# Dropping waits in the attention periods and spreading the weight sums of a threshold attention and squared-ReLU kernel

## The chip, the core and the metric

The kernel runs on one core of a Trainium2 chip. The metric is the device time of one execution in microseconds, given as the median of several runs. The engines of the core work side by side, each through its own queue in order: TensorE (PE in the profile, PEld its weight loads), VectorE (DVE), ScalarE (ACT), GpSimd (POOL), and SyncE (SP), which issues DMAs.

## The reference

Attention of 8 batches with 8 heads, sequences of 576 rows and heads of 64, in float32: scores are q kᵀ / 8; scores below the row's maximum less tau (0.02) are masked; then the softmax and the product with v. The heads' outputs side by side are x, 4608 rows of 512. Then comes a feed-forward block:

```
h = np.maximum(x @ w_in, 0.0)      # w_in 512 x 2048
out = h * h @ w_out                # w_out 2048 x 512
```

## The kernel before

Both weights come as float64; the kernel converts them to float32 itself. Three stages follow one another.

**Attention.** Two heads of a batch make a pair, 32 pairs in all. A pair has four units of 128 query rows, and the last 64 rows of two neighbouring pairs make a shared ninth unit, the rest unit (`units`, 276; in it `t == FULL`). So there are 144 units, and `period(p)` (618) works on two of them at a time, A = 2p and B = 2p + 1, in a software pipeline: p runs from -2 to 74 (1046), with scores and softmax of units in period p and their product with v two periods later. A period is a list of named steps, written by hand: `PLAIN` (593) from p = 35 on, `CONVERTING` (596) for 2 to 34, in which the weights are fetched and converted. Each engine's queue gets its instructions in the order of the list. The steps that matter here:

- `SA`, `SB`: scores of A and of B on PE (`scores`, 423; line 434), 512 main columns and 64 rest columns per head. They are written to the six banks of the PSUM tile `sc`: the main columns of a unit with an even number to banks 0 and 5, of an odd one to 2 and 3, the rest columns to 1 and 4.
- `topA1` and so on: row minima of the negated scores on VectorE (452). `leastA`, `leastB`: the threshold, a tiny operation on POOL (459). `powA0` and so on: the exponentials on ScalarE (462). `maskA0` and so on: mask and row sum on VectorE (467), which waits for `leastA` or `leastB`. `over` (474, POOL) and `inv` (477, VectorE): the reciprocal of the sums. `spread` (517, POOL) widens it.
- `U`, `V`, `W` and `eU`, `eV`, `eW`: transposes of the weights on PE (379) and their copies on ScalarE (524). `W` and `eW` use banks 2 and 3 of `sc`.
- `PV` (533): the product with v on PE, into the start of banks 0 and 5. `x` (652 on VectorE, 654 on ScalarE) takes it from there, `xs` (669, POOL) scales the second half and stores it to DRAM as xT.
- `T` and `eT`: some of the next pairs' q or k rows are transposed on PE (397) into banks 1 and 4 and evicted by ScalarE (402 and 410) into the buffers qT, kT and qR. `TURNS` (487) says in which period. qT has a ring of 3 buffers (`Q_RING`), kT and qR of 4 (`K_RING`). A rest unit reads qR and kT, other units qT and kT.
- `s1`, `s2`: one step each of the sums of the weights (`sums_step`, 571), on POOL: `s1` in every plain period, `s2` in even ones.

**Which waits are kept.** The framework orders any two instructions that it takes to meet in a buffer. Since all attention PSUM is one tile, `touch` (354) is called for each instruction on it, and takes the order away from pairs on different banks (`declare_no_dep`), unless they may meet in SBUF: `MEET` (352) names such kinds. There, a pair of kinds with keys (numbers of pairs) that differ by a multiple of one of the rings named keeps its wait. Before the change, scores and the evictions of turned rows are one kind each, and they keep their wait if the keys differ by a multiple of 3 or of 4.

**Sums.** The feed-forward block multiplies by a recursive scheme with 7 products in place of 8, used twice: 49 products of quarter-sized blocks of blocks, whose operands are sums of blocks. For w_in these are 44 sums of 128x512 tiles in the buffer `wall` (`sums`, 249), as a generator that makes one sum each time it is asked. For the first 512 tokens, x needs 12 more (`prepare_x`, 790), loaded from DRAM in periods 40 to 43 (`load_x`, 762, called in 1048). Before the change these 12 come behind the 44.

**Hidden layers.** Nine steps of 512 tokens (`hidden_layer`, 829), each of 49 products on PE (841) with the combinations on VectorE and POOL (125) and the squares on ScalarE; g is stored to DRAM. After each product a tick comes, 49 in a layer (`also`, 1150). In ticks, `chain_out` (1115) also makes the sums of w_out: 44 chains, each a load, four small subtractions on POOL (122, by `minus`) at its ticks 6 to 9 and a store at tick 10; `CHAINS` (1069) gives their starts, six ticks apart. Their SBUF is loaded over by `load_g` (1140) at the start of the last layer, and `reload` (1058) then brings the sums of w_out into `wall`.

**Output layers.** Nine more steps with 49 products each (976).

Of the kernel before, what the change touches and what calls it, by code (L numbers as in the profile page):

```python
# [14 lines left out]
AF = mybir.ActivationFunctionType  # L15
# [33 lines left out]
def kernel(  # L49
# [25 lines left out]
    nc = tc.nc  # L75
# [5 lines left out]
    FULL = S // P  # L81
# [3 lines left out]
    BANK = 512  # L85
    MAIN = FULL * P
    STEP = 512
    NSTEP = B * S // STEP
# [149 lines left out]
    def convert6(m):  # L238
# [7 lines left out]
        if m >= 16:  # L246
            nc.sync.dma_start(out=slot_of(*chunks[m][1:3]), in_=a.bitcast(FP32))

    def sums(W, which, at):

        first = [at[a][b] for a in range(2) for b in range(2)]

        def inner(m, kinds):
            for op, o, x, y in kinds:
                to = W[m, o] if o == y else weight_tile(W, m, o)
                yield op(nc.gpsimd, to[:, :], W[m, x][:, :], W[m, y][:, :])

        early = which[0:3]
        for m in (1, 2):
            yield from inner(m, early)  # L260
        for op, o, x, y in which:
            for k_ in first:
                to = W[o, k_] if o == y else weight_tile(W, o, k_)
                yield op(nc.gpsimd, to[:, :], W[x, k_][:, :], W[y, k_][:, :])
        for m in OUTER:
            yield from inner(m, which[3:] if m in (1, 2) else which)

# [12 lines left out]
    NU = len(units)  # L280
# [68 lines left out]
    behind = mybir.DependencyInfo(mybir.DependencyClass.Sync, mybir.DependencyReason.DATA)  # L349

    Q_RING, K_RING, W_RING = 3, 4, 2
    MEET = (("scores", "turned", (Q_RING, K_RING)), ("values", "weights", (W_RING,)), ("x", "weights", (W_RING,)))

    def touch(what, made, at, size, key=0):

# [34 lines left out]
    def turn(i, which, spots, other=None):  # L390

        nat, to = loaded.pop((i, which)), places(i)
        of = [nat[:, t, :] for t in range(FULL)] + ([loaded.pop((i, 2))] if which else [])
        for t, x in enumerate(of):
            for r, (spot, at) in enumerate(spots):
                rows = ds(r * HALF, HALF)
                made = nc.tensor.transpose(spot[:, ts(t, HALF)], x[rows, :], ident[rows, rows])
                touch("turns", made, at, BANK)
        half = FULL * HALF

        def scaled(to, spot):
            touch("turned", nc.scalar.activation(out=to, in_=spot[0], func=AF.Identity, scale=qscale[:, :]), spot[1], BANK, i)  # L402

        def then():
            part = lambda r, x, n: (spots[r][0][:, ds(x, n)], spots[r][1])
            if which:
                for r, n in ((0, half), (1, half + REST)):
                    spot = part(r, 0, n)
                    copy_by = other if r and other else nc.scalar.copy
                    touch("turned", copy_by(to[1][:, ds(r * half, n)], spot[0]), spot[1], BANK, i)  # L410
# [12 lines left out]
    def scores(n, rest):  # L423

        of, t = units[n]
        at_k, count = (MAIN, REST) if rest else (0, MAIN)
        for j in range(2):
            first = n % 2 != j
            to = (3 * j + 1) * BANK + first * (BANK - REST) if rest else (3 * j + 2 * first) * BANK
            for c in range(2):  # L430
                rows, at = ds(j * D, D), ds(c * HALF, HALF)
                qT, kT, qR = turned[of[c]]
                lhs = qT[rows, ds((c * FULL + t) * HALF, HALF)] if t < FULL else qR[rows, :]
                made = nc.tensor.matmul(  # L434
                    sc[at, ds(to, count)], lhs, kT[rows, ds(at_k, count)], start=True, stop=True
                )
                touch("scores", made, to, count, of[c])

    def softmax(n):

# [69 lines left out]
    def widen(m):  # L510

        if m not in wT:
            wT[m] = sb.tile([P, (2 * CH + 2) * P], FP32, tag="wT", bufs=W_RING, name="wT")
        one = smalls.pop(m)[:, 3, 0:1]
        wide = bass.AP(tensor=one.tensor, offset=one.offset, ap=[one.ap[0], [1, 2], [2, 2], [0, D]])
        to = wT[m][:, ds(SCALE_AT * P, 2 * P)].rearrange("p (j u d) -> p j u d", j=2, u=2)
        nc.gpsimd.tensor_copy(out=to, in_=wide)
# [42 lines left out]
    def has(n):  # L560
        return 0 <= n < NU
# [4 lines left out]

    def sums_due(p):

        return p > max(starts) and not converts(p)

    def sums_step():
        while summing and next(summing[0], 0) == 0:
            summing.popleft()

    def ask(every=True):

# [7 lines left out]
    def converts(p):  # L584
        return is_wide and (has_chunk(p) or has_chunk(p - 1))
# [4 lines left out]
    def begun(n):  # L590
        return starts.get(n)

    PLAIN = """
        fetch U SA topA1 over s1 s2 topA0 SB topB1 inv eU powA1 V topB0 leastA spread PV powA0 maskA1 leastB maskA0 eV T powB1 x maskB1 powB0 xs maskB0 eT W eW
    """.split()
    CONVERTING = """
        fetch c1 T SA topA1 c3 topA0 U eU powA1 SB topB0 over topB1 powA0 c4 powB0 PV eT inv leastA maskA1 x powB1 leastB spread V eV maskA0 W maskB0 c5 c6 eW maskB1 xs c2
# [20 lines left out]
    def period(p):  # L618
# [66 lines left out]
        def every(key):  # L685
# [12 lines left out]
            "s1": lambda: sums_due(p) and sums_step(), "s2": lambda: sums_due(p) and p % 2 == 0 and sums_step(), "fetch": lambda: fetch(begun(p + 2)),  # L698
        }
        steps["spread"] = lambda: has(2 * m + 2) and widen(m + 1)  # L700
        for times in (4, 8, 14):
            steps[f"id{times}"] = lambda times=times: keep_busy(times)
        steps["over"] = lambda: do(a, "over")
# [314 lines left out]
    with tc.manual_schedule():  # L1018
        with ExitStack() as stack:
# [26 lines left out]
            for p in range(-2, NU // 2 + 3):  # L1046
                period(p)
                if X_FIRST <= p < X_FIRST + 4:
                    load_x(0, XPARTS[p - X_FIRST :][:1])
                if p == X_FIRST + 4:  # L1050
                    summing.append(prepare_x(0, lambda op, out, x, y: op(nc.gpsimd, out, x, y)))
            for _ in range(60):
                sums_step()
            ask()
        b_pool = ctx.enter_context(tc.tile_pool(name="b", bufs=2, space=PSUM))
        banks = ctx.enter_context(tc.tile_pool(name="banks", bufs=1, space=PSUM))
# [9 lines left out]
        halves_ = [(m, k, h) for m, k in blocks_out[EARLY:] for h in range(2)]  # L1066
        chains = [((0, RAW.index(k)), c) for k in RAW for c in range(4)]
        chains += [((1, made_at(m)), c) for c in range(4) for m in OUTER]
        CHAINS = [49 * n + 6 * c for n in range(NSTEP - 1) for c in range(n == 0, 6)][0 : len(chains)]
        QUARTER = BANK // 4  # L1070
        two = lambda t: t.rearrange("p (k o) -> p k o", k=2)
        raw_out = {}
# [61 lines left out]
        for n in range(NSTEP):  # L1134
# [14 lines left out]

            def also(m, at):  # L1150
                i = OUTER.index(m)
                convert_out(n, 7 * i + at)
                chain_out(n, 7 * i + at)
                if not last:
                    if 2 <= i <= 5 and at < 6:
                        next(xsums)
                    return
                spread(work.get(i, []), at)
                if 7 * i + at > 9:
                    reload(7 * i + at - 10)  # L1160
# [80 lines left out]
```

## Time and profile before

| what | value |
|---|---|
| median of 3 runs | 1295.47 us (1295.32 to 1295.79) |
| profiled execution | 1293.22 us, its span 1291.4 us |
| granted TensorE clock | 1.000 |
| PE busy | 1259.7 us, 98% of the span |
| VectorE / ScalarE / POOL busy | 996.2 / 855.5 / 909.8 us |
| DMA | 192.05 MB, mean 149 GB/s |

The span runs from the first to the last instruction. A row of the timeline gives start, length, engine, line, operation, output<-input, and count; what stands in brackets is the engine's idle time before it and what ended that. A row of the groups gives line, engine, operation, shapes and count, then busy time in us and the mean of one in ns, then idle time before and what ended it. A row of busy time by stretch gives the stretch and its length, then for PE, PEld, VectorE, ScalarE and POOL the busy us with the number of instructions, then the clock, the share of the DMA engines and GB/s. A row of waits gives who waited for whom, total us, how often, and the longest.

### The profile page before, as it was taken

How to read it: one execution, taken by the hardware profiler on the slowest of the kernel's cores; microseconds unless marked ns; L12 is line 12 of the kernel's file. 1: busy time of each engine (PE TensorE's matmuls, PEld its weight loads, DVE VectorE, ACT ScalarE, POOL GpSimd, SP SyncE). 2: the span in 40 equal slices, each digit the busy share in tenths (PEclk: the TensorE clock that was granted, in tenths of full speed). 3: DMA queues.
4: the chain of work that ended last, by engine and by line, in shares of the span. 5: the costliest groups of instructions: out<-in, count | busy, mean ns of one | idle time of the engine just before them, and what ended most of it. 6: DMA issues, size and time to landing. Idle time of an engine off the chain costs nothing.

```text
span 1291.4 us, 46350 instructions
## 1 busy us (share of the span) xinstructions
PE 1259.7 (98%) x18627; PEld 1124.3 (87%) x18627; DVE 996.2 (77%) x2425; ACT 855.5 (66%) x1536; POOL 909.8 (70%) x1102
## 2 busy tenths in 40 slices
PE   8999999999999999999999999999999999999998
PEld 6666666667676668999999999999999999999998
DVE  6999999999999995787788778777745654665463
ACT  6999999999999994756675667576523432343240
POOL 2566565666666664887898789668777867776775
PEclk9999999999999999999999999999999999999999
DMA  6555666534333423556655665489545314422411
GB/s 157 148 146 155 166 188 187 147 87 111 88 79 88 97 43 87 185 172 212 199 185 180 214 196 173 149 320 387 197 149 164 106 63 160 164 83 86 160 34 34
DMA packets 247032, 192.05 MB, mean 149 GB/s; under 512 B 97184, under 2 KB 195488, under 8 KB 246816
## 3 DMA queue, kind: packets, MB, share of 16 engines
q1 hardware_dynamic: 245360, 188.63, 48.5%
q8 instruction: 147, 2.41, 0.8%
q10 hardware_dynamic: 1456, 0.44, 0.1%
q14 instruction: 69, 0.57, 0.1%
HBM read 116.65 MB, written 72.35 MB: 146 GB/s over the span
## 4 chain that ended last, share of the span: by engine, by line
PE 61%; ACT 1%; DVE 1%; DMA 0%; issue 0%; POOL 0%; ACTq 0%; DVEq 0%; POOLq 0%
PE ph L841 30%; PE po L976 29%; PE sc L533 1%; PE sc L434 1%; DMA g<-arena 0%; ACT c L787 0%; ACT arena L820 0%; ACT arena L821 0%; PE pt L379 0%; ACT arena L524 0%; DVE arena L452 0%; DVE arena L125 0%; DVE arena L122 0%; POOL arena L122 0%; DVE arena L467 0%
## 5 line engine op out<-in xcount | busy, mean ns | idle before, releaser
L125 POOL TENSOR_TENSOR arena<-arena 128x512 f32<-128x512 f32 (+1 forms) x314 | 378.0, 1224 | 122.7 <-DVE arena L125 105.9
L976 PE MATMUL po<-wall,arena 128*128 128x128 f32 x3528 | 394.7, 275 | 1.4 <-ACT arena L753 1.4
L976 PEld LDWEIGHTS po<-wall,arena 128*128 128x128 f32 x3528 | 394.3, 192 | 1.8 <-ACT arena L753 1.8
L841 PE MATMUL ph<-arena,wall 128*128 128x128 f32 x3528 | 394.2, 275 | 0.5 <-DVE arena L652 0.5
L841 PEld LDWEIGHTS ph<-arena,wall 128*128 128x128 f32 x3528 | 394.0, 192 | 0.6 <-ACT arena L654 0.6
L125 DVE TENSOR_TENSOR arena<-ph,arena 128x512 f32<-128x512 f32 x378 | 256.5, 689 | 86.1 <-PE ph L841 65.7
L122 POOL TENSOR_TENSOR arena<-arena 128x128 f32<-128x128 f32 (+2 forms) x314 | 255.1, 814 | 52.4 <-DMA arena<-w 36.3
L462 ACT ACTIVATE arena<-arena 128x576 f32<-128x576 f32 x288 | 228.4, 889 | 21.2 <-DVE arena L452 21.2
L125 DVE TENSOR_TENSOR arena<-po,arena 128x128 f32<-128x128 f32 x378 | 108.5, 290 | 168.6 <-PE po L976 164.4
L467 DVE SCALAR_TENSOR_TENSOR arena<-arena 128x576 f32<-128x576 f32 x288 | 227.3, 818 | 2.9 <-POOL arena L459 2.0
L452 DVE TENSOR_SCALAR_CACHE_REDUCE arena<-sc 128x576 f32<-128x576 f32 x288 | 204.6, 752 | 14.5 <-ACT arena L524 6.9
L787 ACT COPY c<-arena 128x512 f32<-128x512 f32 (+1 forms) x303 | 173.9, 581 | 49.4 <-DVE arena L122 41.2
L533 PEld LDWEIGHTS sc<-arena 64*64 64x64 f32 x5760 | 144.4, 133 | 44.3 <-DVE arena L452 42.2
L122 DVE TENSOR_TENSOR arena<-arena,c 128x512 f32<-128x512 f32 (+1 forms) x267 | 175.1, 664 | 5.6 <-ACT c L787 4.0
L434 PE MATMUL sc<-arena 64*64 64x64 f32 (+1 forms) x2304 | 168.0, 414 | 4.6 <-ACT arena L402 2.7
L533 PE MATMUL sc<-arena 64*64 64x128 f32 (+1 forms) x5760 | 160.5, 262 | 10.1 <-DVE arena L452 6.1
L524 ACT COPY arena<-pt 128x1024 f32<-128x1024 f32 x144 | 161.7, 1123 | 2.0 <-PE pt L379 1.9
L753 ACT COPY arena<-po 128x128 f32<-128x128 f32 x63 | 16.7, 265 | 186.7 <-PE po L976 183.9
L379 PEld LDWEIGHTS pt<-ident,arena 64*128 64x128 f32 x2304 | 83.1, 138 | 43.1 <-ACT arena L524 35.1
L753 ACT COPY arena<-ph 128x512 f32<-128x512 f32 x63 | 36.7, 582 | 122.0 <-PE ph L841 121.5
L434 PEld LDWEIGHTS sc<-arena 64*64 64x64 f32 x2304 | 60.6, 133 | 52.5 <-issue 26.3
L379 PE MATMUL pt<-ident,arena 64*128 64x64 f32 x2304 | 100.8, 227 | 4.0 <-ACT arena L524 3.6
(49 smaller groups left out, 962.7 us busy)
## 6 DMA issues: line engine op xcount, KB each, us to landing
g<-arena SPq DMA_DIRECT2D x144, 256.0 KB, 2.7
arena<-g SPq DMA_DIRECT2D x144, 256.0 KB, 4.3
w<-arena SPq DMA_DIRECT2D x60, 256.0 KB, 2.4
wall<-w SPq DMA_DIRECT2D x49, 256.0 KB, 5.2
arena<-w SPq DMA_DIRECT2D x44, 256.0 KB, 3.6
arena<-in_v_dram SPq DMA_DIRECT2D x32, 288.0 KB, 3.9
out_dram<-arena SPq DMA_DIRECT2D x70, 128.0 KB, 3.0
arena<-in_q_dram SPq DMA_DIRECT2D x64, 128.0 KB, 3.8
```

The source lines that it names most:

```text
L122: e.tensor_tensor(out=out, in0=x, in1=y, op=ALU.subtract)
L125: e.tensor_tensor(out=out, in0=x, in1=y, op=ALU.add)
L379: made = nc.tensor.transpose(pt[:, r, ts(slot, HALF)], of[rows, :], ident[rows, rows])
L434: made = nc.tensor.matmul(sc[at, ds(to, count)], lhs, kT[rows, ds(at_k, count)], start=True, stop=True)
L452: made = nc.vector.tensor_scalar(out=s[:, j, :], in0=sc[:, ds(at, S)], scalar1=1.0, scalar2=None, op0=ALU.mult, op1=ALU.min, accum_out=nmx ...
L462: nc.scalar.activation(out=w[:, :, j, :], in_=of(j), func=AF.Exp, bias=nmx[:, j : j + 1], scale=-1.0)
L467: nc.vector.scalar_tensor_tensor(out=w[:, :, j, :], in0=of(j), scalar=thr[:, j : j + 1], in1=w[:, :, j, :], op0=ALU.is_le, op1=ALU.mult, a ...
L524: touch("weights", nc.scalar.copy(joined(to), whole(pt, 0, count)), at, 2 * BANK, m)
L533: made = nc.tensor.matmul(sc[ds(u * D, D), ds(5 * j * BANK + row, count)], loaded_v[i][rows, (c - (u != j)) % CH, :], wT[m][rows, ds(weigh ...
L787: nc.scalar.copy(c, y)
L841: nc.tensor.matmul(to[:, j, :], W_IN[m, k][:, ts(j, P)], of[k][:, m - 1, :], start=(not more and j == 0), stop=True, skip_group_check=True,)
L976: nc.tensor.matmul(to, g[:, j, :], w[:, j, :], start=(not more and j == 0), stop=(j == 3), skip_group_check=True)
```

## The change

It has three parts. The kinds are told apart: scores of a unit that reads qT are "q scores" and those of a rest unit "scores"; evictions are "turned q" or "turned k" (kT and qR). Each pair of kinds keeps its wait only by the ring that it really shares, and "scores" with "turned q" none. The plain list loses `s2`, so POOL makes one sum in each period from 35 to 71, and the 12 sums of x go ahead of what is left of the 44. Of those, 25 are then made in the periods; four more are made by VectorE in period 72 behind `inv` (`sV`), four by VectorE after that period, and the last 11 by POOL in the first hidden layer, in ticks 0 to 6, 9, 12, 15 and 18. The chains of the first hidden layer start at tick 18 instead of 6, two fewer in that layer, and all later ones come two places (twelve ticks) later.

```diff
+    by = [nc.gpsimd]
...
-                yield op(nc.gpsimd, to[:, :], W[m, x][:, :], W[m, y][:, :])
+                yield op(by[0], to[:, :], W[m, x][:, :], W[m, y][:, :])
...
-    MEET = (("scores", "turned", (Q_RING, K_RING)), ("values", "weights", (W_RING,)), ("x", "weights", (W_RING,)))
+    MEET = (("q scores", "turned q", (Q_RING,)), ("scores", "turned k", (K_RING,)), ("q scores", "turned k", (K_RING,)), ("values", "weights", (W_RING,)), ("x", "weights", (W_RING,)))
...
+        kind = "turned k" if which else "turned q"
...
-                touch("scores", made, to, count, of[c])
+                touch("q scores" if t < FULL else "scores", made, to, count, of[c])
...
-        return p > max(starts) and not converts(p)
-
-    def sums_step():
-        while summing and next(summing[0], 0) == 0:
-            summing.popleft()
+        return max(starts) < p < NU // 2 and not converts(p)
+
+    def sums_step(e=nc.gpsimd, times=1):
+        by[0] = e
+        for _ in range(times):
+            while summing and next(summing[0], 0) == 0:
+                summing.popleft()
...
-        fetch U SA topA1 over s1 s2 topA0 SB topB1 inv eU powA1 V topB0 leastA spread PV powA0 maskA1 leastB maskA0 eV T powB1 x maskB1 powB0 xs maskB0 eT W eW
+        fetch U SA topA1 over s1 topA0 SB topB1 inv sV eU powA1 V topB0 leastA spread PV powA0 maskA1 leastB maskA0 eV T powB1 x maskB1 powB0 xs maskB0 eT W eW
...
+        last = p == NU // 2
+        steps["sV"] = lambda: last and sums_step(nc.vector, 4)
...
+                if p == NU // 2:
+                    sums_step(nc.vector, 4)
                 if p == X_FIRST + 4:
-                    summing.append(prepare_x(0, lambda op, out, x, y: op(nc.gpsimd, out, x, y)))
-            for _ in range(60):
-                sums_step()
+                    summing.appendleft(prepare_x(0, lambda op, out, x, y: op(nc.gpsimd, out, x, y)))
...
-        CHAINS = [49 * n + 6 * c for n in range(NSTEP - 1) for c in range(n == 0, 6)][0 : len(chains)]
+        CHAINS = [49 * n + 6 * c for n in range(NSTEP - 1) for c in range(3 if n == 0 else 0, 6)][0 : len(chains)]
...
+                tick = 7 * i + at
+                if n == 0 and (tick < 7 or tick % 3 == 0):
+                    sums_step()
+                assert tick < 27 or not summing
```

More of the change, by code (lines that the diff above doesn't have):

```diff
@@ L263, in sums @@
                 to = W[o, k_] if o == y else weight_tile(W, o, k_)
-                yield op(nc.gpsimd, to[:, :], W[x, k_][:, :], W[y, k_][:, :])
+                yield op(by[0], to[:, :], W[x, k_][:, :], W[y, k_][:, :])
         for m in OUTER:
@@ L399, in turn @@
         half = FULL * HALF
+        kind = "turned k" if which else "turned q"
         def scaled(to, spot):
-            touch("turned", nc.scalar.activation(out=to, in_=spot[0], func=AF.Identity, scale=qscale[:, :]), spot[1], BANK, i)
+            touch(kind, nc.scalar.activation(out=to, in_=spot[0], func=AF.Identity, scale=qscale[:, :]), spot[1], BANK, i)
         def then():
@@ L409, in then @@
                     copy_by = other if r and other else nc.scalar.copy
-                    touch("turned", copy_by(to[1][:, ds(r * half, n)], spot[0]), spot[1], BANK, i)
+                    touch(kind, copy_by(to[1][:, ds(r * half, n)], spot[0]), spot[1], BANK, i)
                 scaled(to[2], part(0, half, REST))
@@ L697, in period @@
             "c5": lambda: convert5(begun(p - 1)), "c6": lambda: convert6(begun(p - 1)),
-            "s1": lambda: sums_due(p) and sums_step(), "s2": lambda: sums_due(p) and p % 2 == 0 and sums_step(), "fetch": lambda: fetch(begun(p + 2)),
+            "s1": lambda: sums_due(p) and sums_step(), "fetch": lambda: fetch(begun(p + 2)),
         }
         steps["spread"] = lambda: has(2 * m + 2) and widen(m + 1)
+        last = p == NU // 2
+        steps["sV"] = lambda: last and sums_step(nc.vector, 4)
         for times in (4, 8, 14):
```

## The prediction

> **What bounds the kernel now.** I read the page first, for the engines' shares, then the busy time by stretch, then the waits of TensorE, and last the timeline at single periods.
>
> ```profile
> span 1291.4 us, 46350 instructions
> PE 1259.7 (98%) x18627; PEld 1124.3 (87%) x18627; DVE 996.2 (77%) x2425; ACT 855.5 (66%) x1536; POOL 909.8 (70%) x1102
> ```
> ```profile
> 252.35:482.97 230.62, 223.60 (x5747) 160.40 (x5743) 218.84 (x647) 214.70 (x363) 152.42 (x236) 1.00 0.37 86
> 497.40:541.00 43.60, 43.60 (x391) 43.60 (x392) 33.21 (x53) 23.50 (x43) 30.63 (x39) 1.00 0.49 149
> 848.00:892.00 44.00, 44.00 (x397) 44.00 (x396) 31.81 (x48) 26.23 (x48) 30.31 (x25) 1.00 1.02 375
> ```
>
> TensorE (PE) is busy 1259.7 of 1291.4 us, so 31.7 us is all that taking waits away could win. The first stretch is the 36 plain attention periods (p = 35 to 70): PE works 223.60 of 230.62 us there and idles 7.0. The other two are the first and the last hidden layer, where PE never stops: nothing can be won there, only lost. So the change is judged in the plain periods, and its costs are sought wherever it puts work.
>
> A period starts when PE begins the scores of unit A (line 434):
>
> ```profile
> 252.35 2.18 PE L434 MATMUL sc<-arena 64*64 64x512 f32 x32
> ...
> 284.83 2.18 PE L434 MATMUL sc<-arena 64*64 64x512 f32 x32 [0.67 <-ACT arena L402]
> 291.12 2.33 PE L434 MATMUL sc<-arena 64*64 64x512 f32 x32
> 297.19 2.18 PE L434 MATMUL sc<-arena 64*64 64x512 f32 x32
> 303.76 2.18 PE L434 MATMUL sc<-arena 64*64 64x512 f32 x32 [0.18 <-DVE arena L652]
> 310.05 2.33 PE L434 MATMUL sc<-arena 64*64 64x512 f32 x32
> ...
> 482.97 2.18 PE L434 MATMUL sc<-arena 64*64 64x512 f32 x32 [0.33 <-DVE arena L652]
> ```
> ```profile
> PE sc L434 <- ACT arena L402: 2.7, 4, 0.7
> PE sc L434 <- DVE arena L652: 1.6, 7, 0.3
> ```
>
> The second fence holds PE's waits in the plain periods, all of them: four of about 0.67 us on ScalarE's eviction of turned q rows (402), and seven of up to 0.33 us on VectorE's x (652), which reads bank 0 before scores overwrite it. From 284.83 to 291.12 is 6.29 us, from 303.76 to 310.05 again 6.29: the length when PE waits for nothing and turns rows. From 291.12 to 297.19, where nothing is turned, it is 6.07. These are PE's floors. Rows are turned up to p = 67, except in 41, 50 and 59, so of the 36 periods 30 have the first floor and 6 the second: 188.7 + 36.4 = 225.1 us against 230.6. **At most 5.5 us** is to be had by that count, and by all idle time 7.0.
>
> **Part 1: the waits.** 284.83 starts p = 40, whose unit A is the shared rest unit of pairs 16 and 17. The q rows turned just before are those of pair 19: 19 - 16 = 3, a multiple of Q_RING, so the old rule keeps a wait. But a rest unit reads qR and kT, not qT, and its first matmuls write banks 0 and 5, not the banks 1 and 4 that the eviction empties. The same meeting comes once in nine plain periods, at p = 40, 49, 58 and 67: the four waits above.
>
> ```profile
> 283.50 0.66 PE L379 MATMUL pt<-ident,arena 64*128 64x64 f32 x16
> ```
> ```profile
> 283.95 0.83 ACT L402 ACTIVATE arena<-sc,qscale 128x256 f32<-128x256 f32 x2
> ```
> ```profile
> 283.59 0.28 DVE L652 TENSOR_TENSOR arena<-sc,arena 128x128 f32<-128x128 f32 x1
> ```
>
> The eviction ends at 284.78, and PE starts 0.05 later. Next in line are PE's own transposes, done at 284.16, and x, done at 283.87; so the scores can start at 284.17, 0.66 earlier. The rest columns in banks 1 and 4, a real meeting, follow their 512-column matmuls by 0.9 us, after 284.78. The new rule drops the old wait and keeps qT by 3 and kT by 4. Four times 0.66 is **-2.6 us**; bounds 0 (the wait is another) and -2.7.
>
> **Part 2: one sum a period.** POOL makes two sums in even periods and one in odd ones, between the small operation `over` and the threshold `leastA`, for which VectorE's first mask waits.
>
> ```profile
> 305.59 1.28 POOL L122 TENSOR_TENSOR wall<-wall 128x512 f32<-128x512 f32 x1
> ...
> 311.65 2.52 POOL L122 TENSOR_TENSOR wall<-wall 128x512 f32<-128x512 f32 x2
> 314.15 0.29 POOL L459 TENSOR_SCALAR arena<-arena,tau_p 128x2 f32<-128x2 f32 x1
> ```
> ```profile
> 305.23 0.76 DVE L452 TENSOR_SCALAR_CACHE_REDUCE arena<-sc 128x576 f32<-128x576 f32 x1
> 308.01 0.81 DVE L467 SCALAR_TENSOR_TENSOR arena<-arena 128x576 f32<-128x576 f32 x1
> 311.51 0.76 DVE L452 TENSOR_SCALAR_CACHE_REDUCE arena<-sc 128x576 f32<-128x576 f32 x1 [0.27 <-ACT arena L524]
> 314.48 0.92 DVE L467 SCALAR_TENSOR_TENSOR arena<-arena 128x576 f32<-128x576 f32 x1
> ```
>
> In the odd period 43 the mask starts 2.78 us after the first row minimum (305.23 to 308.01), and VectorE has 0.27 us free before the next minimum. In the even period 44 it starts 2.97 after (311.51 to 314.48), just behind `leastA`, and takes 0.92 instead of 0.81: 0.3 us late, as much as VectorE had free. Then x is late, and PE waits at 652. All seven of those waits stand at the end of an even period; of these the fences show 303.76 (after 42) and 482.97 (after 70). With one sum every period should run like an odd one. The visible waits are 1.6 us, the rest up to the ceiling 5.5 - 2.6 = 2.9. Odd periods are not all at the floor, so I take **-2.4 us**; bounds 0 (VectorE stays late for another reason) and -2.9, with all idle time -4.3.
>
> **What is late next.** The twelve x sums move ahead of the weight sums, to p = 45 to 56. Their last load is issued by the period before:
>
> ```profile
> 316.33 0.54 SPq L774 DMA_DIRECT2D arena<-xT  x1
> ```
> ```profile
> DMA to landing us min/median/max: 3.2/3.6/4.0
> ```
> ```profile
> 318.22 1.28 POOL L122 TENSOR_TENSOR wall<-wall 128x512 f32<-128x512 f32 x1
> 319.48 0.29 POOL L459 TENSOR_SCALAR arena<-arena,tau_p 128x2 f32<-128x2 f32 x1
> ...
> 320.82 0.79 POOL L459 TENSOR_SCALAR arena<-arena,tau_p 128x2 f32<-128x2 f32 x1 [0.22 <-DVE arena L452]
> ```
> ```profile
> 320.64 0.81 DVE L467 SCALAR_TENSOR_TENSOR arena<-arena 128x576 f32<-128x576 f32 x1
> ```
>
> Landing is at 316.33 + 3.6 = 319.9, and the first x sum needs that very part, where a weight sum now starts at 318.22. POOL, in order, holds `leastA`, the copy that widens the reciprocals and `leastB` behind it: `leastA` ends at 319.9 + 1.28 + 0.29 = 321.5 instead of 319.8, the mask starts then instead of at 320.64, 0.9 late, of which VectorE's slack takes 0.2. **+0.7 us** once; bounds 0 (an earlier landing) and 1.1 (landing after 4.0). SP's queue gets no other step in these periods.
>
> **Part 3: the boundary.** Eight sums go to VectorE, four after the reciprocal of p = 72 and four after the x of that period. Behind them in its queue stand the two last x (652); the last one frees the banks for which the first hidden product waits.
>
> ```profile
> 490.73 0.18 DVE L477 RECIPROCAL arena<-arena 128x4 f32<-128x4 f32 x1 [0.36 <-POOL arena L474]
> 493.47 0.29 DVE L652 TENSOR_TENSOR arena<-sc,arena 128x128 f32<-128x128 f32 x1 [2.56 <-PE sc L533]
> 496.93 0.29 DVE L652 TENSOR_TENSOR arena<-sc,arena 128x128 f32<-128x128 f32 x1 [3.17 <-PE sc L533]
> ```
> ```profile
> L125 DVE TENSOR_TENSOR arena<-ph,arena 128x512 f32<-128x512 f32 x378 | 256.5, 689 | 86.1 <-PE ph L841 65.7 <-ACT arena L753 5.4 <-POOL arena L125 4.7
> ...
> L125 DVE TENSOR_TENSOR arena<-arena 128x128 f32<-128x128 f32 x3 | 0.9, 293 | 0.2
> ```
>
> The trace has no 128x512 sum on VectorE with both inputs in SBUF. The nearest row has one from PSUM, 0.69 us; above it stands POOL's 1.28. I take 0.69. Four are 2.76 against 2.56 free, and the next four 2.76 against 3.17; together 5.5 against 5.7. **+0.1 us**; bounds 0 and, by 1.28, 10.2 - 5.7 = +4.5.
>
> ```profile
> 491.72 0.40 POOL L517 COPY arena<-arena 128x256 f32<-128x256 f32 x1
> ...
> 493.80 0.46 POOL L669 TENSOR_TENSOR arena<-arena 128x128 f32<-128x128 f32 x1 [1.68 <-ACT arena L654]
> ```
>
> Something speaks against this place. `leastB` at 320.82 takes 0.79 us beside VectorE's masks, which read two inputs in SBUF as the sums would; the same operation at 319.48 takes 0.29. If the sums and POOL's two operations above stand in each other's way, VectorE loses up to 0.40 + 0.46 = 0.9: 6.4 against 5.7, +0.7 instead of +0.1. The Trainium skill, "SBUF — State Buffer", section "Who interferes with whom", has this as a rule: a VectorE instruction with two SBUF inputs and a GpSimd instruction that reads SBUF exclude each other, whichever starts first. The trace agrees with that, 0.79 against 0.29.
>
> **Part 4: the first hidden layer.** Eleven sums go to POOL there, seven in the first seven ticks and four at ticks 9, 12, 15 and 18, and two chains of four small subtractions leave it for the end of layer 8.
>
> ```profile
> 508.24 1.27 POOL L125 TENSOR_TENSOR arena<-arena 128x512 f32<-128x512 f32 x1 [10.47 <-DVE arena L125]
> ```
> ```profile
> L122 POOL TENSOR_TENSOR arena<-arena 128x128 f32<-128x128 f32 x176 | 80.6, 459 | 42.0 <-DMA arena<-w 36.3
> ```
> ```profile
> L841 PE MATMUL ph<-arena,wall 128*128 128x128 f32 x3528 | 394.2, 275 | 0.5 <-DVE arena L652 0.5
> ```
>
> POOL stands idle for 10.47 us up to its first addition of the layer: room for seven sums of 1.28 (9.0). The other four are 5.1 us where eight subtractions of 0.46 (3.7) leave; the 1.4 more fits into what is left of the stretch's idle time, 43.6 - 30.6 - 10.5 = 2.5. Nine layers take 394.2 us, so one takes 43.8 and a tick, a forty-ninth of it, 0.89; the weights made here are first read at tick 28, ten ticks after the last sum. **0 us**; the cover is POOL's idle time, and without it the four sums would cost up to 5.1. The chains, twelve ticks later, end at tick 34 of the eighth layer, 13 us before the last layer's loads. 0 as well.
>
> **Sum:** -2.6 - 2.4 + 0.7 + 0.1 = -4.2 us. The profiled execution took 1293.22 us, its span 1291.4; the median of the runs shown is 1295.47, 2.25 more. I take the difference as the same on both: 1289.0 for the profiled one, **1291.3 us** for the median.
>
> **Rivals.**
> *VectorE stays the bound.* If even periods are long for another reason (rows turned, ACT's copies), part 2 gives nothing: -2.6 + 0.8 = -1.8, 1293.7 us. For it: VectorE is busy 218.84 of 230.62 us. Against it: the 0.27 us free in odd periods. Chance 0.14.
> *The wait stays.* If the four waits are no ring waits, or another takes their place at once, only part 2 is left: -2.4 + 0.8 = -1.6, 1293.9 us. Against it: pairs 16 and 19, banks 0 and 5, and just four of them. Chance 0.08.
> *Products wait for sums.* The other side: the old rule shows that waits are kept between instructions which touch different places of one buffer. If the tensor `wall`, which POOL now writes while PE reads it, does the same, each product of the first 19 ticks waits for the sum issued beside it. Seven of 1.28 in seven ticks of 0.89 cost 9.0 - 6.2 = 2.8, four more up to 5.1: -4.2 + 7.9 = +3.7, 1299.2 us. It ends slower from 4.2 us of such waits on. Against it: in the last hidden layer DMAs reload this tensor under PE, which is busy 44.00 of 44.00 us. Chance 0.08.
> *The boundary.* If VectorE and POOL stand in each other's way there, +0.7 instead of +0.1: -3.6, 1291.9 us. For it: 0.79 against 0.29 for `leastB`. Against it: what POOL does there is short and off VectorE's queue for most of the 5.7 us. Chance 0.04. This is what the Trainium skill's rule, cited in part 3, would give.
>
> **How the numbers follow.** The forecast has 0.66, its own range 1290.0 (the ceiling 5.5) to 1292.5. The range 1289.8 to 1294.2 reaches over the first two rivals and leaves out the slower one. A measurement tells about 0.2%, 2.6 us, from no change: forecast and boundary count as faster, 0.70; the first two rivals as same, 0.22; the third as slower, 0.08.
>
> **What would show it.** Right: no wait of 434 on 402 among PE's waits of the plain periods; few on 652; 226 us instead of 230.6 from p = 35 to p = 71; one mask 0.9 late at p = 45; 0.69 for the eight sums; PE without a pause in the first hidden layer. Wrong: PE waiting in 841 for POOL, a last x later than its PV, or plain periods that still alternate.

## The result and the profile after

The changed kernel takes 1290.93 us in the median of 6 runs (1288.99 to 1292.73), the kernel before 1295.63 in 6 runs beside them (1294.82 to 1298.75). The ratio is 0.996 with a 95% interval of 0.9946 to 0.9975, so some 3 to 7 us less. The forecast was 1291.3.

The page of the changed kernel, its span and the busy time of the engines:

```profile
span 1290.4 us, 46352 instructions
PE 1261.3 (98%) x18627; PEld 1127.2 (87%) x18627; DVE 998.5 (77%) x2433; ACT 854.9 (66%) x1536; POOL 897.4 (70%) x1094
```

This profiled execution took 1292.20 us, only 1.0 less than that of before, though the medians lie 4.7 apart. So the spans of the two must not be compared as wholes; the trace has to be read by stage. Lines after the change: 402 is now 406, 434 is 438, 459 is 463, 467 is 471, 517 is 521, 652 is 658, 841 is 849; in the experiments made from the kernel before (waits alone, second sum late, two sums in every period) those from 434 to 652 stand two further on, such as 436, 461, 469 and 654. The plain periods 35 to 70 and the first hidden layer, by the view of busy time by stretch:

```profile
256.12:481.79 225.67, 224.52 (x5746) 162.41 (x5742) 216.27 (x647) 214.29 (x362) 126.64 (x218) 1.00 0.38 88
496.20:540.00 43.80, 43.80 (x392) 43.80 (x393) 33.37 (x53) 23.64 (x43) 41.01 (x42) 1.00 0.40 124
```

The plain stretch fell from 230.62 to 225.67 us: **4.95 us less**; no other stage got shorter by more than 0.02. PE idles 1.15 us there (225.67 - 224.52) where it idled 7.0. In the first hidden layer POOL now works 41.0 us and PE still never stops. PE's waits in the plain stretch, all of them, and three starts of periods (39, 40 and 42):

```profile
PE sc L438 <- DVE arena L658: 0.2, 1, 0.2
```
```profile
281.25 2.33 PE L438 MATMUL sc<-arena 64*64 64x512 f32 x32
287.48 2.31 PE L438 MATMUL sc<-arena 64*64 64x512 f32 x32
...
299.84 2.18 PE L438 MATMUL sc<-arena 64*64 64x512 f32 x32
```

No wait on the eviction is left, and one of 0.2 us on x where there were seven. Period 39 lasts 6.23 us (281.25 to 287.48) instead of 6.98.

Where the rest of the profiled execution's time went: periods 1 to 34, whose code the change hardly touches, took 242.17 us (13.95 to 256.12) instead of 238.78. PE's waits there name one part of the cause, loads of q and k rows that land late:

```profile
PE sc L399 <- DMA arena<-in_q_dram: 2.1, 4, 1.1
...
PE sc L399 <- DMA arena<-in_k_dram: 0.4, 1, 0.4
```

The profile of before has no such wait. The other part is the granted clock, the share of its full speed at which TensorE is let run. Period 31 of the changed kernel, and a piece of it, by the view of busy time by stretch, where the clock is the third number from the end:

```profile
225.69:233.29 7.60, 7.50 (x146) 5.13 (x145) 4.67 (x16) 5.61 (x12) 3.71 (x7) 0.78 0.90 248
226.83:230.24 3.41, 3.41 (x48) 1.96 (x43) 1.55 (x5) 2.21 (x4) 1.34 (x4) 0.50 0.88 241
```

For 3.41 us TensorE ran at half speed, and the period took 7.60 us where it took 6.28 before, at a clock of 1.00. Over the twelve kernels profiled here, all with nearly the same code in this stage, it took 238.8 to 242.4 us, and before happened to be the shortest of all. Most of that spread goes with the clock in periods 1 and 2: they took 13.6 us in the three executions with a clock of 1.00 there, 15.0 to 15.1 in the five with 0.89, and 16.4 to 16.5 in the four with 0.79. The other 32 periods took 225.1 to 225.9 us in ten of the twelve, 227.3 with sixteen sums on VectorE and 228.6 in the changed kernel.

### The profile page after: what moved, and what is told of

Its sections match the earlier page's. It is cut to its first block, busy times and chain, and to the rows that moved or that the text cites. A ratio compares the mean times of both kernels' runs of the same rounds, so it can differ in the third digit from the quotient of the medians.

```text
span 1290.4 us, 46352 instructions
## 1 busy us (share of the span) xinstructions
PE 1261.3 (98%) x18627; PEld 1127.2 (87%) x18627; DVE 998.5 (77%) x2433; ACT 854.9 (66%) x1536; POOL 897.4 (70%) x1094
## 4 chain that ended last, share of the span: by engine, by line
PE 64%; DMA 2%; DVE 1%; ACT 1%; issue 0%; POOL 0%; SPq 0%; ACTq 0%; DVEq 0%; POOLq 0%
PE ph L849 30%; PE po L984 29%; PE sc L537 2%; PE sc L438 2%; DMA wall<-w 1%; PE pt L381 1%; DMA g<-arena 0%; PE sc L381 0%; PE sc L399 0%; DVE arena L456 0%; ACT c L795 0%; ACT arena L528 0%; DVE arena L125 0%; DVE arena L122 0%; POOL arena L125 0%
## 5 line engine op out<-in xcount | busy, mean ns | idle before, releaser
L849 PE MATMUL ph<-arena,wall 128*128 128x128 f32 x3528 | 394.4, 275 | 0.5 <-DVE arena L658 0.5
L466 ACT ACTIVATE arena<-arena 128x576 f32<-128x576 f32 x288 | 224.3, 858 | 16.7 <-DVE arena L456 16.7
L537 PEld LDWEIGHTS sc<-arena 64*64 64x64 f32 x5760 | 144.8, 133 | 44.3 <-DVE arena L456 40.4
L438 PE MATMUL sc<-arena 64*64 64x64 f32 (+1 forms) x2304 | 170.6, 417 | 0.3 <-DVE arena L658 0.2
L528 ACT COPY arena<-pt 128x1024 f32<-128x1024 f32 x144 | 157.4, 1093 | 3.6 <-PE pt L381 3.6
L438 PEld LDWEIGHTS sc<-arena 64*64 64x64 f32 x2304 | 62.8, 133 | 47.0 <-issue 22.6
```

The source lines that it names most:

```text
L438: made = nc.tensor.matmul(sc[at, ds(to, count)], lhs, kT[rows, ds(at_k, count)], start=True, stop=True)
L466: nc.scalar.activation(out=w[:, :, j, :], in_=of(j), func=AF.Exp, bias=nmx[:, j : j + 1], scale=-1.0)
L528: touch("weights", nc.scalar.copy(joined(to), whole(pt, 0, count)), at, 2 * BANK, m)
L537: made = nc.tensor.matmul(sc[ds(u * D, D), ds(5 * j * BANK + row, count)], loaded_v[i][rows, (c - (u != j)) % CH, :], wT[m][rows, ds(weigh ...
L849: nc.tensor.matmul(to[:, j, :], W_IN[m, k][:, ts(j, P)], of[k][:, m - 1, :], start=(not more and j == 0), stop=True, skip_group_check=True,)
```

## The experiments

The theory: two separate gains in the plain periods, one from four needless waits, one from a second POOL sum that holds the threshold back; everything else is covered. The rivals are those of the prediction. All plain stretches below run from the start of period 35 to that of period 71, read from each kernel's trace as above; before has 230.62 and after 225.67. Each is of one execution; four kernels that have the same code up to the end of the stretch (the changed one, sixteen sums, nineteen sums, chains not shifted) agree to 0.5 us. The medians of the whole kernel are coarser: by them alone, sums alone is not told from before, as its interval reaches 1.0003. So what each part is worth is read from the stretch.

| kernel | plain stretch, us | median us, and of before on the same chip | ratio to before (95%) |
|---|---|---|---|
| waits alone | 227.78 | 1294.21, 1296.39 | 0.9983 (0.9971 to 0.9995) |
| sums alone | 228.59 | 1295.42, 1296.39 | 0.999 (0.9978 to 1.0003) |
| x sums two periods later | 225.24 | 1291.66, 1296.39 | 0.9959 (0.9945 to 0.9974) |
| second sum late in the period | 236.89 | 1304.47, 1296.39 | 1.0068 (1.005 to 1.0085) |
| sixteen sums on VectorE | 225.67 | 1298.39, 1296.63 | 1.0014 (1.0001 to 1.0027) |
| nineteen sums in the layer | 225.15 | 1299.39, 1296.63 | 1.0021 (1.0008 to 1.0035) |
| chains not shifted | 225.35 | 1292.13, 1296.63 | 0.9969 (0.9955 to 0.9983) |
| two sums in every period | 234.07 | 1300.76, 1296.63 | 1.0036 (1.0023 to 1.0049) |
| no sum in even periods | 225.11 | 1316.26, 1295.09 | one run |
| one wait back | 229.99 | 1295.55, 1295.09 | one run |

**Waits alone.** Only the kinds and `MEET`:

```diff
-    MEET = (("scores", "turned", (Q_RING, K_RING)), ...
+    MEET = (("q scores", "turned q", (Q_RING,)), ("scores", "turned k", (K_RING,)), ("q scores", "turned k", (K_RING,)), ...
```

> The kernel before with the new kinds of waits alone; all sums stay where they were. My theory (two separate gains): periods 39, 48, 57 and 66 shrink from 6.98 to 6.23-6.33 us, the even ones keep their excess, plain stretch about 227.8 us instead of 230.6, time 2.6 to 3.0 us below before. Rival (one gain in two places: VectorE or ScalarE is the bound and takes the stall's place): the four periods shrink but the ones behind them grow, less than 1 us is left.

PE's waits in the plain stretch, all of them:

```profile
PE sc L436 <- DVE arena L654: 1.6, 7, 0.3
```

The waits on the eviction are gone, all seven on x stay, 1.6 us as before. The four periods last 6.23 to 6.34 us, the stretch is 2.84 us shorter: the first theory, to the tenth.

**Sums alone.** The changed kernel with the old rule put back:

```diff
-    MEET = (("q scores", "turned q", (Q_RING,)), ("scores", "turned k", (K_RING,)), ...
+    MEET = (("scores", "turned", (Q_RING, K_RING)), ...
...
-        kind = "turned k" if which else "turned q"
+        kind = "turned"
...
-                touch("q scores" if t < FULL else "scores", made, to, count, of[c])
+                touch("scores", made, to, count, of[c])
```

> The changed kernel with the old rule for the waits: the four waits of 434 on 402 are back, the sums are moved as in the change. My theory: four periods of 6.98 us stay, even periods run like odd ones, period 45 loses 0.3 us to the load of x; about 1.7 to 2.2 us below before. Rival (even periods were long for another reason): even periods keep their excess and the time is that of before, within 0.5 us.

```profile
PE sc L438 <- ACT arena L406: 2.7, 4, 0.7
PE sc L438 <- DVE arena L658: 0.4, 1, 0.4
```

Now the waits on the eviction are back, and those on x fall to one. The stretch is 2.03 us shorter than before. 2.84 + 2.03 = 4.87 against 4.95 for both: the two gains add up, as separate ones must.

**One wait back.** Of all that the change drops, one pair of kinds with one ring put back:

```diff
-    MEET = (... ("scores", "turned k", (K_RING,)), ("q scores", ...
+    MEET = (... ("scores", "turned k", (K_RING,)), ("scores", "turned q", (Q_RING,)), ("q scores", ...
```

> The changed kernel with one of the dropped pairs of kinds put back: scores of a rest unit and evicted q rows, by 3. My theory (the four waits are this pair's alone): periods 39, 48, 57 and 66 are 6.97 or 6.98 us again and PE waits four times 0.67 us on the eviction, plain stretch 228.3 to 228.7, as with all the old waits. Rival (other dropped pairs, scores of other units by 4 or k rows by 3, carry part of it): some of the four periods stay short.

```profile
PE sc L438 <- ACT arena L406: 2.7, 4, 0.7
```

Periods 39, 48, 57 and 66 last 6.97 or 6.98 again. The stretch, 229.99, is above what was expected, because period 35 took 7.63 us instead of 6.15 in this one execution, with a granted clock of 0.78:

```profile
254.99:262.62 7.63, 7.63 (x156) 4.85 (x152) 5.66 (x17) 5.13 (x8) 5.29 (x8) 0.78 0.31 80
```

Without that it is 228.5. So the cost of the old rule was this one pair: a rest unit's scores, which never read qT, against an eviction into qT.

**X sums two periods later.**

```diff
-                if p == X_FIRST + 4:
+                if p == X_FIRST + 6:
```

> The changed kernel with the sums of x starting two periods later (47 instead of 45), all else equal. My theory (POOL waits at 45 for the last load of x and holds the threshold behind it): that wait of 1.5 us of POOL is gone, period 45 falls from 6.56 to about 6.30, 0.3 us below the changed kernel. Rival (period 45 is long for another reason, such as the rows turned in it): 6.56 stays and so does the time.

Period 45 of the changed kernel, on POOL, VectorE and PE in turn:

```profile
321.73 1.28 POOL L122 TENSOR_TENSOR arena<-arena 128x512 f32<-128x512 f32 x1 [1.47 <-DMA arena<-xT]
322.99 0.29 POOL L463 TENSOR_SCALAR arena<-arena,tau_p 128x2 f32<-128x2 f32 x1
```
```profile
323.31 0.92 DVE L471 SCALAR_TENSOR_TENSOR arena<-arena 128x576 f32<-128x576 f32 x1 [0.30 <-POOL arena L463]
```
```profile
325.24 1.09 PE L438 MATMUL sc<-arena 64*64 64x512 f32 x8 [0.19 <-DVE arena L658]
```

POOL waits 1.47 us for the load, the threshold comes behind the sum, the mask behind the threshold, x behind the mask, and PE 0.19 us behind x. In the experiment period 45 lasts 6.29 us instead of 6.56. The stretch is 0.43 shorter: 0.27 in period 45, and 0.14 in period 61, which this edit does not touch (6.63 against 6.77). Its ratio is the lowest of all, but by less than these runs can tell from the changed kernel (0.9959 against 0.996).

**Second sum late in the period.** With the new waits, all sums stay on POOL in the periods; only the second one moves behind the last product of x:

```diff
-        fetch U SA topA1 over s1 s2 topA0 SB ... xs maskB0 eT W eW
+        fetch U SA topA1 over s1 topA0 SB ... xs s2 maskB0 eT W eW
```

> The kernel before with the new waits, and with the second sum of the even periods kept on POOL but moved from ahead of the threshold to behind the last product of x (after xs); no sum is moved to VectorE or into the hidden layer. Theory of place (the second sum costs only because the threshold of unit A stands behind it in POOL's queue): even periods run like odd ones, 225.5 to 226 us for the plain stretch, 0 to 0.5 us below the changed kernel. Rival, by the exclusion of VectorE's two-input masks and POOL's sums: the sum now lies beside the masks of unit B, which grow by up to 1 us in each even period, and most of part 2 is lost again, 1 to 3 us above the changed kernel.

The last two masks of an even period on VectorE, and the sum on POOL:

```profile
320.81 0.81 DVE L469 SCALAR_TENSOR_TENSOR arena<-arena 128x576 f32<-128x576 f32 x1
...
321.55 1.82 DVE L469 SCALAR_TENSOR_TENSOR arena<-arena 128x576 f32<-128x576 f32 x1
```
```profile
320.96 1.79 POOL L122 TENSOR_TENSOR wall<-wall 128x512 f32<-128x512 f32 x1
```

The sum takes 1.79 us instead of 1.28, and the second mask 1.82 instead of 0.81. The ends fit instructions that take turns, to within 0.2 us: counted back from its end at 322.75, the sum's 1.28 us begin at 321.47, about when the first mask ends; and the second mask, issued at 321.55, ends 0.62 after the sum does, where it needs 0.81 alone. That agrees with the rule of the Trainium skill, "SBUF — State Buffer", section "Who interferes with whom": a VectorE instruction with two SBUF inputs and a GpSimd one that reads SBUF exclude each other. I had the sign of it and far too small a size. Most even periods run at the floor now, but the odd ones behind them last 6.7 to 7.3 us, and the stretch is 11.2 us longer than the changed kernel's. PE's waits in it, all of them, add up to just that:

```profile
PE sc L535 <- DVE arena L454: 11.2, 17, 0.7
```

The row minima (454) come late behind the long mask, and PE's product with v (535) waits for them, because it writes over scores that they read: of the microsecond that the mask loses, up to 0.7 us reaches PE, in each of the 17 odd periods from 37 to 69. A second sum cannot simply be moved within the period: while VectorE takes row minima out of PSUM it is harmless but holds the threshold, and later it lies on the masks.

**Two sums in every period.** With the new waits:

```diff
-            ... "s2": lambda: sums_due(p) and p % 2 == 0 and sums_step(), ...
+            ... "s2": lambda: sums_due(p) and sums_step(), ...
```

> The kernel before with the new waits and two sums in every plain period until they run out (p = 35 to 62), instead of in even ones. If each second sum costs its own 0.1 to 0.3 us, 27 periods lose 3 to 6 us against one sum each. If, as I read the trace, VectorE becomes the bound by the late threshold and the longer first mask, 6.3 us of work in a period of 6.29, all periods get about 6.33 to 6.40 whether rows are turned or not, and the periods without turning lose most (6.07 to 6.35): 1 to 2.5 us above one sum each for the plain stretch, 226.3 to 227.8 us.

A whole period, from first mask to first mask, on VectorE and then on POOL:

```profile
332.91 0.92 DVE L469 SCALAR_TENSOR_TENSOR arena<-arena 128x576 f32<-128x576 f32 x1 [0.31 <-POOL arena L461]
...
335.44 0.81 DVE L469 SCALAR_TENSOR_TENSOR arena<-arena 128x576 f32<-128x576 f32 x1
...
339.59 0.92 DVE L469 SCALAR_TENSOR_TENSOR arena<-arena 128x576 f32<-128x576 f32 x1 [0.43 <-POOL arena L461]
```
```profile
336.35 0.23 POOL L476 TENSOR_SCALAR arena<-arena 128x4 f32<-128x4 f32 x1 [1.47 <-DVE arena L469]
336.66 1.27 POOL L125 TENSOR_TENSOR wall<-wall 128x512 f32<-128x512 f32 x1
338.01 1.28 POOL L122 TENSOR_TENSOR wall<-wall 128x512 f32<-128x512 f32 x1
339.27 0.29 POOL L461 TENSOR_SCALAR arena<-arena,tau_p 128x2 f32<-128x2 f32 x1
```

My size was wrong, 234.07 us instead of at most 227.8, and so was the account of it as VectorE's work. (About 1.1 us of the 234.07 is period 35, 7.27 us long at a granted clock of 0.82.) From period 38 to 58 every one lasts 6.45 to 6.68 us, turning or not, and the rows show why: it is a closed loop. Masks from 332.91 to 336.25, `over` to 336.58, the sums to 339.29, the threshold to 339.56, the next mask at 339.59. Both sums stand in it in full; VectorE is not full but waits for POOL. With one sum the loop is 1.3 us shorter, 5.4, and disappears under PE's 6.29. In the kernel before, the rows shown in the prediction are those of the same loop: first masks at 308.01 and 314.48, 6.47 apart, with the two sums from 311.65 and the threshold from 314.15 between them. Even periods had the long loop, and odd ones caught up.

**No sum in even periods.** The changed kernel, with what is left of the sums made in one go ahead of the hidden layers:

```diff
-            "s1": lambda: sums_due(p) and sums_step(), ...
+            "s1": lambda: sums_due(p) and p % 2 == 1 and sums_step(), ...
...
+            for _ in range(60):
+                sums_step()
```

> The changed kernel with no sum at all in even plain periods; what is left of the sums is made by POOL in one go ahead of the hidden layers, so that only the plain stretch is to be read and the whole takes some 30 us more. My theory (the loop from the last mask of a period over POOL's sums and the threshold to the first mask of the next is hidden under PE with one sum and not with two): even periods stay what they are with one sum, 6.23 to 6.32 with turning and 6.07 without, plain stretch 225.0 to 225.7. Rival (each sum costs its share): even periods lose another 0.1 to 0.3 us each, plain stretch 221 to 224.

Even periods last what they last with one sum: 6.29 to 6.36 for 36, 38, 42, 46 and 54 in both kernels, 6.07 for 50. The stretch is 225.11 us, and 225.24 in the kernel that lacks only the stop at 45. So the first sum of a period costs nothing and the second does: a threshold, not a price per sum.

**Sixteen sums on VectorE.**

```diff
-        steps["sV"] = lambda: last and sums_step(nc.vector, 4)
+        steps["sV"] = lambda: last and sums_step(nc.vector, 8)
...
-                    sums_step(nc.vector, 4)
+                    sums_step(nc.vector, 8)
```

> The changed kernel with sixteen sums on VectorE at the boundary instead of eight, eight ahead of each of the two last x; three are left for the hidden layer. In the changed kernel's profile the eight lie 0.66 us apart and VectorE is free for 5.7 us. My theory (they cost nothing until that free time is used up, and then all of it): 16 x 0.66 = 10.6 us, so the last x and the first hidden product come 4.6 us later, 4 to 5 us above the changed kernel. Rival (VectorE's sums are hidden, since the hidden products do not wait for the last x): 0 us.

PE at the boundary in this kernel, the last PV and the first hidden product:

```profile
493.73 3.63 PE L537 MATMUL sc<-arena 64*64 64x128 f32 x108 [2.38 <-DVE arena L658]
499.37 0.80 PE L849 MATMUL ph<-arena,wall 128*128 128x128 f32 x5 [2.02 <-DVE arena L658]
```

PE now stops twice for VectorE's x. From the start of period 71 to the first hidden product it is 19.30 us (480.07 to 499.37) against 14.40 (481.79 to 496.19): 4.9 more, where 4.6 was expected. The last PV takes 3.63 us here instead of 2.33, at a granted clock of 0.60, but that does not lengthen the boundary: VectorE, for which PE waits again behind it, works without a pause from 487.9 to 499.2. By the ratios the whole is some 7 us above the changed kernel; 2.3 of that lies in the hidden layers (396.7 against 394.4 us). PE waits 0.5 us in them, and for 3.4 us the granted clock was half:

```profile
500.10:503.50 3.40, 3.40 (x18) 3.40 (x17) 0.69 (x1) 0.59 (x1) 2.77 (x3) 0.50 0.40 78
```

Half of that, 1.7 us, makes up the rest by my estimate. It is not the sums' own price, unless the stops of PE bring the low clock with them, which is not shown.

**Nineteen sums in the layer.**

```diff
-        steps["sV"] = lambda: last and sums_step(nc.vector, 4)
+        steps["sV"] = lambda: None
...
-                if p == NU // 2:
-                    sums_step(nc.vector, 4)
...
-                if n == 0 and (tick < 7 or tick % 3 == 0):
+                if n == 0 and tick < 20:
```

> The changed kernel with no sum on VectorE: nineteen sums on POOL in the first hidden layer, one behind each of the first nineteen ticks. My theory (POOL's idle time of some 10.5 us at the layer's start is the cover, and what goes beyond it delays additions, whose six temporary tiles run out, then VectorE, then PE): POOL is some 9 us late by tick 20, PE stops in the second and third outer step of the layer for the first time, 4 to 8 us above the changed kernel. Rival (POOL's lateness in this layer is taken up by its queues and buffers): less than 1 us. Rival of the waits on the whole weight buffer: PE stops from tick 0 on, at POOL's pace of 1.28 a tick.

PE in the first hidden layer, which starts at 495.71, and VectorE's waits on POOL there:

```profile
520.17 1.16 PE L849 MATMUL ph<-arena,wall 128*128 128x128 f32 x8 [0.76 <-DVE arena L125]
523.43 5.62 PE L849 MATMUL ph<-arena,wall 128*128 128x128 f32 x48 [2.10 <-DVE arena L125]
530.37 4.84 PE L849 MATMUL ph<-arena,wall 128*128 128x128 f32 x41 [1.31 <-DVE arena L125]
```
```profile
DVE arena L125 <- POOL arena L125: 7.7, 4, 2.6
```

The chain is the expected one, POOL late, then VectorE, then PE, though an outer step later than I had put it: PE first stops 24.5 us into the layer, in the fourth outer step. Together with one stop in the next layer PE waits 4.8 us; the hidden layers last 401.3 us (495.71 to 896.98), 6.9 more; where the other 2.1 us lie is left open. (The boundary is 16.07 us long in this execution instead of 14.40, at a granted clock of 0.89; x sums two periods later has the same, 16.06 at 0.89.) PE runs through the first 24 us while POOL writes the weights beside it, which ends the rival of products that wait for sums.

**Chains not shifted.**

```diff
-        CHAINS = [... for c in range(3 if n == 0 else 0, 6)][0 : len(chains)]
+        CHAINS = [... for c in range(n == 0, 6)][0 : len(chains)]
```

> The changed kernel with the chains where they were before, starting at tick 6 of the first hidden layer, so that POOL has eight more subtractions of 0.46 us there beside the eleven sums: 41.0 + 3.7 = 44.7 us of work in a layer of 43.8. My theory: POOL ends the layer some 3 us later than in the changed kernel and takes it from the idle start of the next layer; PE does not stop, or for less than 1 us; the time is that of the changed kernel within 1 us. Rival (POOL is at its limit there and the shift was needed): PE stops, 2 to 4 us above.

All of PE's waits in the hidden layers on VectorE's sums:

```profile
PE ph L849 <- DVE arena L125: 0.3, 1, 0.3
```

PE waits 0.3 us, and the hidden layers last 0.7 us longer than the changed kernel's (395.1 against 394.4) in this execution; the ratio, 0.9969 against 0.996, does not tell the two apart.

## Why the prediction was right

**Part 1**, forecast -2.6: measured -2.84 alone. The four periods give 2.68 of it (0.64 to 0.75 each), and the kernel with one wait back shows that it is the pair named.

**Part 2**, forecast -2.4: measured -2.03 alone, and that includes what period 45 loses in it (6.74 instead of 6.29), so about -2.5 before that. The step holds, its account only in part. I had put it down to VectorE being 0.3 us late with just 0.3 free; the kernel with two sums everywhere shows a loop through two engines, in which VectorE's own free time plays no part. Read that way, the rows of that kernel give the period directly: 3.3 us of masks and x, 2.6 of sums, 0.7 of small operations and the steps between.

**What is late next**, forecast +0.7: measured +0.27 in the changed kernel's profile (6.56 against 6.29) and 0.45 with the sums alone; in the seven kernels whose sums of x begin there, period 45 took 6.39 to 6.74 us. The chain of waits is the one forecast, link by link. The term was too large in the changed kernel because the load landed sooner: it was issued at 318.73 and POOL went on at 321.73, so 3.0 us where I had taken 3.6; the first mask started 0.4 us late and not 0.9.

**The boundary**, forecast +0.1: 14.40 us from period 71 to the hidden layers in both kernels, so 0. VectorE's queue there:

```profile
489.64 2.06 DVE L122 TENSOR_TENSOR wall<-wall 128x512 f32<-128x512 f32 x3
491.63 0.68 DVE L125 TENSOR_TENSOR wall<-wall 128x512 f32<-128x512 f32 x1
492.30 0.29 DVE L658 TENSOR_TENSOR arena<-sc,arena 128x128 f32<-128x128 f32 x1
492.51 2.14 DVE L122 TENSOR_TENSOR wall<-wall 128x512 f32<-128x512 f32 x3
494.57 0.68 DVE L125 TENSOR_TENSOR wall<-wall 128x512 f32<-128x512 f32 x1
495.76 0.29 DVE L658 TENSOR_TENSOR arena<-sc,arena 128x128 f32<-128x128 f32 x1 [0.51 <-issue]
```

Eight sums 0.66 to 0.71 apart, and 0.51 us free before the last x, which follows PE's last PV: the cover holds, and with sixteen sums it is used up as counted. POOL's two operations beside them:

```profile
489.86 0.70 POOL L521 COPY arena<-arena 128x256 f32<-128x256 f32 x1 [0.34 <-DVE arena L481]
492.63 0.87 POOL L675 TENSOR_TENSOR arena<-arena 128x128 f32<-128x128 f32 x1 [2.07 <-ACT arena L660]
```

They take 0.70 and 0.87 instead of 0.40 and 0.46. So the two engines do stand in each other's way, as that rival had it, but POOL pays, and nobody waits for POOL here. The rival was wrong about who pays.

**The first hidden layer**, forecast 0: POOL's queue there:

```profile
496.55 3.85 POOL L122 TENSOR_TENSOR wall<-wall 128x512 f32<-128x512 f32 x3
500.36 1.28 POOL L125 TENSOR_TENSOR wall<-wall 128x512 f32<-128x512 f32 x1
501.72 3.85 POOL L122 TENSOR_TENSOR wall<-wall 128x512 f32<-128x512 f32 x3
505.52 1.28 POOL L125 TENSOR_TENSOR wall<-wall 128x512 f32<-128x512 f32 x1
507.06 1.28 POOL L125 TENSOR_TENSOR arena<-arena 128x512 f32<-128x512 f32 x1 [0.27 <-DVE arena L125]
```

Eight sums fill what had been idle, and the first addition follows with 0.27 us to spare. With eight more sums the cover is gone and PE stops, so the margin is real and not wide. The nine layers together did lengthen a little, 394.2 us instead of 394.0 to the first output product; the same two times stand in the profiles of one wait back and sums alone on one side, of waits alone, second sum late and two sums in every period on the other. PE shows no wait for it, and what costs the 0.2 us is left open.

**The sum**, forecast -4.2: -4.95 + 0 + 0.2 by stage, -4.7 by the medians. By stage, the terms that were off most are the late load, 0.4 too large, and the waits, 0.2 too small. That the median came out within 0.4 us of the forecast is luck in part, as the interval of the runs is some 4 us wide. What I did not foresee is that the profiled execution of before was a short one in a stage that the change leaves alone: the forecast for the profiled execution, 1289.0, was missed by 3.2 us, about what periods 1 to 34 lost there to late loads and a lower clock. The difference of 1.0 between the two profiled executions would have misled anyone who read spans only.

## What to carry to other kernels

When a framework's waits are kept by a rule, look for waits that come exactly as often as the rule and the real sharing differ: four equal gaps at every ninth period named the pair before any experiment did. Work that an engine does between receiving one signal and sending the next is part of a loop, and its price is nothing up to a point and full beyond it; add up the loop, not the engine's load. Before work is moved, see what its new neighbours read: here the same sum is free beside row minima out of PSUM and costs a microsecond beside masks out of SBUF.

## What the runs showed of the hardware that was not expected

The size of the exclusion: beside each other a POOL sum of 1.28 us and a VectorE mask of 0.81 end after 1.79 and 1.82 us, so the mask loses a whole microsecond, more than the stop of PE that the sum was moved to avoid. And how much of the spread goes with the granted clock: it falls to 0.50 for 3.41 us, or two or three times that, near 20 us in nine of the twelve profiles and else at places that differ from one execution to the next. Such a fall made period 31 of the changed kernel 7.60 us long instead of 6.28, period 35 with one wait back 7.63 instead of 6.15, and the boundary of two experiments 16.1 instead of 14.4; it makes the first 34 periods of nearly the same code last up to 3 us longer, as much as most of the change is worth. Late loads add to that, most in two of the twelve profiles. The runs of one kernel spread by 3 to 8.5 us, and the clock goes with it there too: of the 24 runs of before that stand beside the first four experiments, those with a clock of 1.000 have a median of 1293.2 us (4 runs), those with 0.999 one of 1295.5 (6), with 0.998 one of 1296.2 (5) and with 0.997 one of 1297.9 (6). What makes the clock fall is not shown.
